# Twelve early loads moved from GpSimd's casting DMA queue to two plain fp32 queues, with the casts on ScalarE and VectorE

## The chip, the core and the metric

The kernel runs on one core of a Trainium2 chip. The metric is the time of one execution in microseconds of device time; lower is better. The core's engines run side by side, each through its own list of instructions in order: TensorE (PE, the matmuls), VectorE (DVE), ScalarE (ACT), GpSimd (POOL) and SyncE (SP). Sixteen DMA engines move data between the chip's main memory and the core. A transfer is started by an instruction on SP, ACT or POOL and goes through that engine's queue. In the profile q0 is POOL's queue, q1 SP's and q10 ACT's.

## What is computed

Retention (attention without a softmax, with a decay by distance) for 8 batches and 8 heads, and a feed-forward network with an exact GELU on its result:

```python
# q, k, v: (8, 8, 576, 64) fp32; w_in: (512, 2048), w_out: (2048, 512)
scores = scale * np.matmul(q, k.transpose(0, 1, 3, 2))
gamma = 1.0 - 2.0 ** (-5.0 - np.arange(H, dtype=np.float32))
Dmat = np.where(rel >= 0, gamma[:, None, None] ** rel[None, :, :], 0.0)
attn = np.matmul(scores * Dmat[None], v)
x = attn.transpose(0, 2, 1, 3).reshape(4608, 512)
h = x @ w_in
g = 0.5 * h * (1.0 + erf(h * inv_sqrt2))
out = g @ w_out
```

## The kernel before

The 4,608 rows of `x` are worked in 36 *units*. A unit is a chunk of 128 positions of one batch with all its heads (the last, short chunks of two batches share a unit). Four units make a block of 512 rows. For each unit the kernel loads q, k and v as bfloat16, turns q and k (`turn`: PE transposes, line 457), forms the scores (`scores`), multiplies them with the decay mask on VectorE (`masked`), multiplies by v (`inner`) and copies the result into a tile `x` (`evacuate`). Across chunks a state is carried (`state`, `cross`). For each block follow the first matmul with `w_in` and the GELU (`mlp1`, `mlp1_fast`) and the second with `w_out` (`mlp2`, `mlp2_fast`). Nearly all matmuls are recorded on line 453, the helper `mm`.

The order of all instructions is fixed when the program is built. A planner in the kernel keeps an estimated clock for each engine (`T`), estimated landing times of loads (`land`, `land_in`, `land_out`), and at each step picks work that is ready by these estimates. On the chip each engine then runs its list in that order and waits on semaphores where an input is not there. Where the planner expects PE to wait, early in the run, it puts in matmuls on a tile of zeros (`warm`, the first ten of them ahead of the loop) that fill the time.

The first four units (chunk 0 of batches 0 to 3) are special: their q, k and v go into slices of one tile, `early`, each [128, 512] bfloat16, and they come first. In the kernel before, three of these twelve tiles (q, k, v of unit 0) are loaded as fp32 at the very start, by SP (q32, first_v) and ACT (k32), line 147, into buffers that later hold outputs (`o_sb`), and are cast to bfloat16 by instructions: q on VectorE (line 1220), k and v on ScalarE (line 1223). The other nine are issued by POOL (line 369), whose DMA casts on the way.

POOL's queue carries nearly everything: `load` issues one item, and the list `ORDER` gives the items' order. `wi0` to `wi7` are the eight chunks of `w_in` (256 columns each, line 311), `wo0` to `wo7` the eight chunks of `w_out` (line 326), `q4` the q of unit 4, `n` a second layout of k, `dq` a table made on POOL, `io` the two iotas of the constants. `sw_dma` is the planner's estimate for POOL's queue: at most eight transfers in flight, each with an issue time and a time to move.

The constants at the top of the kernel steer the planner: how far scores may run ahead of the MLP (`AHEAD`, `RATE`), when units are joined (`JOIN`, `LEAD`, `NEAR`), when the first states and a mask are made (`STATE10`, `MSK_AT`).

Of the kernel before, what the change touches and what calls it, by code (L numbers as in the profile page):

```python
# [9 lines left out]
FP32 = mybir.dt.float32  # L10
# [7 lines left out]
def kernel(  # L18
# [14 lines left out]
    nc = tc.nc  # L33
    ctx.enter_context(tc.manual_schedule())

    B, H, S, D = q.shape
# [5 lines left out]
    C = 128  # L42
# [10 lines left out]
    units = [(bp, 0, j) for bp in range(2) for j in range(2)]  # L53
# [23 lines left out]
    N_LK = 4  # L77
# [4 lines left out]
    N_VH = 4  # L82
    VH_ACT = [4, 22, 1]
    N_XB = 4
    AHEAD = 8
    RATE = 5.6
    STORE_AT = 62.0
    CROWD = 66.0
    STATE10 = 36.0
    HOT = 8.0  # L90
    FETCH = 5.0
    ARRIVE = 5.6
    WARM_TO = 24.0
    JOIN = 1
    JOIN_SB = 0.0
    VISIT = 4
    LEAD = 3.0
    NEAR = 1.4
    SLACK, SB, PER_G, PER_B, TURN0 = 1.2, 2.0, 8.0, 20.0, 0.0
    FINE = 0.38  # L100
    FPOOL = 0.6
    N_V = 6
    V0_HW = 1
    N_WARM = 10
    MSK_AT = 20.0
    HK = N_DF // 2

    const = ctx.enter_context(tc.tile_pool(name="const", bufs=1))
    ld_pool = ctx.enter_context(tc.tile_pool(name="ld", bufs=1))
# [5 lines left out]
    o_pool = ctx.enter_context(tc.tile_pool(name="o", bufs=4))  # L115
# [3 lines left out]
    T = dict.fromkeys(("pe", "act", "dve", "pool", "sp"), 0.0)  # L119
# [22 lines left out]


    first = {}
    for nm, src, eng in (("q32", q, nc.sync), ("k32", k, nc.scalar), ("first_v", v, nc.sync))[:2 + V0_HW]:
        t = first[nm] = o_pool.tile([128, H, D], FP32, tag="o_sb", name=nm)
        eng.dma_start(t, src[0, :, 0:C, :].rearrange("h s d -> s h d"))
    zeros = ld_pool.tile([128, 512], BF16, tag="v", bufs=N_V, name="zeros")
    nc.vector.memset(zeros, 0.0)
    lgh = const.tile([128, H, 1], FP32, name="lgh")  # L150
# [81 lines left out]
    sw = [0.0]  # L232
# [3 lines left out]
    land = {}  # L236
    loaded = {}
    land_in, land_out = {}, {}

    def sw_dma(issue, move):  # L240
        if len(flying) >= 8:
            T["pool"] = max(T["pool"], flying[-8])
        at = T["pool"]
        T["pool"] += issue
        sw[0] = max(sw[0] + move, at + ARRIVE + move - 0.9)
        flying.append(sw[0])
        return sw[0]

# [55 lines left out]
    def load(what, i):  # L304
        if what == "io":
            constants()
            return
        if what == "v" and i == 0 and V0_HW:
            return
        if what == "wi":  # L310
            nc.gpsimd.dma_start(w_in[:, :, i * 256:(i + 1) * 256],  # L311
                                moe_w_in[:, i * 256:(i + 1) * 256].rearrange("(c p) f -> p c f", p=128))
            land_in[i] = sw_dma(0.79, 1.35)
            return
        if what == "dq":
            at, by = (i - 1, step) if i else (1, back)
            assert at in dq_done
            dq_done.add(i)
            finish_later()
            n = min(C, S - i * C)  # L320
            nc.gpsimd.tensor_tensor(dqT[:, i, :, 0:n], dqT[:, at, :, 0:n],
                                    by.to_broadcast([128, HP, n]), op=ALU.mult)
            on("pool", 1.2, 0.0, True)
            return
        if what == "wo":
            nc.gpsimd.dma_start(w_out[:, 2 * i:2 * i + 2, :],
                                moe_w_out[i * 256:(i + 1) * 256, :].rearrange("(c p) f -> p c f", p=128))
            land_out[i] = sw_dma(0.75, 1.36) + 0.5
            return
        if group_of[i] in BY_PE and what == "n":  # L330
            return
        bp, ci, j = units[i]
        qk, v_ld, kn = tiles_of(i)
        if what in "qk" and group_of[i] in BY_PE:
            dst = qk["qk".index(what)].rearrange("p (h e j d) -> p e h j d", h=HP, e=2, j=2)[:, :, :, j]
            for e in range(2):
                nc.gpsimd.dma_start(dst[:, e], {"q": q, "k": k}[what][2 * bp + j, HP * e:HP * e + HP, ci * C:ci * C + C, :].rearrange("h s d -> s h d"))
                land[what, i] = sw_dma(FPOOL, 0.48)
            return
        if what in "qk" and group_of[i] in BY_DVE:  # L340

            n = C if j is not None else TAIL
            per = n // 32 * D
            for jj in (j,) if j is not None else range(2):
                for e in range(2):
                    p0 = 64 * e + 32 * jj
                    nc.gpsimd.dma_start(qk["qk".index(what)][p0:p0 + 32, 0:HP * per].rearrange("p (h x) -> p h x", h=HP),  # L347
                                        {"q": q, "k": k}[what][2 * bp + jj, HP * e:HP * e + HP, ci * C:ci * C + n, :]
                                        .rearrange("h (b t) d -> b h (t d)", b=32))
                    land[what, i] = sw_dma(FPOOL, FINE) if j is not None else sw_dma(FPOOL, FINE / 2)  # L350
            return
        if what == "n":
            nc.gpsimd.dma_start(kn.rearrange("p j e h d -> p (j e h) d"),
                                k[2 * bp:2 * bp + 2, :, ci * C:ci * C + C, :].rearrange("b h s d -> s (b h) d"))
            land[what, i] = land[what, i + 1] = sw_dma(1.27, 1.8)
            return
        if what == "v" and i >= 4 and j is not None:
            nc.gpsimd.dma_start(v_ld.rearrange("p j h d -> p (j h) d"),  # L358
                                v[2 * bp:2 * bp + 2, :, ci * C:ci * C + C, :].rearrange("b h s d -> s (b h) d"))
            land[what, i] = land[what, i + 1] = sw_dma(1.27, 1.8)  # L360
            return
        src = {"q": q, "k": k, "v": v}[what]
        for jj in (j,) if j is not None else range(2):
            n = C if j is not None else TAIL
            if what == "v":
                dst = v_ld if i < 4 else v_ld[:, j] if j is not None else v_ld[n * jj:n * jj + n, 0]
            else:
                dst = qk["qk".index(what)] if i < 4 else qk["qk".index(what)][0:n, :, jj]
            nc.gpsimd.dma_start(dst, src[2 * bp + jj, :, ci * C:ci * C + n, :].rearrange("h s d -> s h d"))
            land[what, i] = sw_dma(0.88, 0.9) if j is not None else sw_dma(0.68, 0.5)  # L370

    tiles_of(0)
    land["q", 0], land["k", 0] = 4.85, 5.5
    if V0_HW:
        land["v", 0] = 6.8
    cast_due = {("q", 0): (loaded[0][0][0], first["q32"]), ("k", 0): (loaded[0][0][1], first["k32"])}
    if V0_HW:
        cast_due["v", 0] = (loaded[0][1], first["first_v"])
    ORDER = ("wi7 io wi0 q1 k2 wi1 k1 k3 v0 v1 q2 wo2 q3 wi5 v2 wo0 wi2 wi3 wi6 v3 wo3 wo4 wi4 wo5 wo1 wo6 n4 q4 "
             "wo7 k4 dq2 v4 k5 q5 q6 q8 q7 k6 k7 v8 v6 k8 k9 q10 n8 n6 k10 k11 q9 dq3 q11 k12 dq0 k13 q12 v12 v10 "  # L380
             "dq4 n10 n12 q13").split()

    def next_order():
        item = ORDER.pop(0)
# [828 lines left out]
    def fire():  # L1213
        now = T["pe"]
        while ORDER and T["pool"] <= now + 1.5:
            next_order()
        for key in [x for x in cast_due if land[x] <= now + 0.2]:
            dst, src = cast_due.pop(key)
            if key[0] == "q":
                nc.vector.tensor_copy(dst, src)  # L1220
                land[key] = on("dve", 0.66, land[key]) + 0.05
                continue
            nc.scalar.copy(dst, src)
            land[key] = on("act", 0.6, land[key]) + 0.05
            if key[0] == "k":
                more_constants()
        while later:
            n = next((n for n, x in enumerate(later) if x[0] <= now and T[x[1]] <= now + 0.05), None)
            if n is None:
                break  # L1230
            _, engine, dur, fn = later.pop(n)
            fn()
            on(engine, dur, now)
        if FAST2 and not wt and not wsum and len(land_out) == N_DF // 2 and max(land_out.values()) <= now and {0, 1, 2, 3} <= s_done:
            wsum.extend(w_out_sums())
        while cast_u and cast_u[0][0] <= now + 0.1:
            state_cast()
        while apart_due and apart_due[0][1] <= now + 0.1 and T["act"] <= now + (0.5 if apart_due[0][0] > group_of[min(nA, N_U - 1)] else 3.0):
            apart()
        while True:  # L1240
            jobs = side_jobs(now)
            if not jobs:
                break
            min(jobs, key=lambda x: x[0])[1]()
        while stores and max(stores[0][0], STORE_AT if stores[0][1] == 0 else 0.0) <= now + 0.2:
            put()
# [52 lines left out]
    for _ in range(N_WARM):  # L1299
        b, t = bank([128, 512], FP32, "warm")  # L1300
# [149 lines left out]
```

## Time and profile before

| | |
|---|---|
| time, median of 2 runs | 290.36 us (289.91 to 290.81) |
| the profiled execution's own time | 290.68 us |
| its span, first to last instruction | 288.8 us |
| PE busy | 279.9 us, 97% |
| DVE, ACT, POOL busy | 228.3, 181.1, 140.8 us |
| POOL's DMA queue | 21.12 MB in 100,528 packets |
| SP's and ACT's DMA queues | 9.51 and 0.72 MB |
| granted clock | 1.000 |

Busy times are sums over the whole span. PE's share includes the matmuls on zeros. A line in the timeline has the start, the length, the engine, the line of the kernel, what is written and read with shapes, the count, and in brackets the idle time before it and what ended it. A DMA queue's row has the number of its packets in the window asked for, their megabytes, and the time that they took as a share of the sixteen engines' time; packets of one queue overlap, so the share can pass 100%.

### The profile page before, as it was taken

The numbers are of one execution on the slowest core, as the hardware profiler recorded it, in microseconds if no ns is written. First come the engines' busy times: TensorE is split into PE (matmuls) and PEld (weight loads), VectorE is DVE, ScalarE is ACT, GpSimd is POOL, SyncE is SP. The second block draws the span as 40 slices with busy tenths as digits, with TensorE's granted clock in tenths as the row PEclk, the third lists the DMA queues.
The fourth block names the chain that finished last, engine by engine and source line by source line (L and its number), as shares of the span: only waits on it lengthen the run. The fifth ranks groups of instructions, "written<-read, shape, count | busy, mean of one in ns | idle before, by whom it ended". The sixth has DMA issues, their size and how long they took to land.

```text
span 288.8 us, 9857 instructions
## 1 busy us (share of the span) xinstructions
PE 279.9 (97%) x4211; PEld 210.2 (73%) x4216; DVE 228.3 (79%) x386; ACT 181.1 (63%) x406; POOL 140.8 (49%) x213
## 2 busy tenths in 40 slices
PE   7899999999999999999999999999999999999994
PEld 3468768788764566666666666777888888888883
DVE  6473297499795689678997799869999999999861
ACT  7556544895758868777787779664545453556421
POOL 8865799798849967878677774000000000000000
PEclk9999999999999999999999999999999999999999
DMA  9999999979998999999999996311020202202014
GB/s 158 168 189 195 190 157 160 207 85 140 130 148 64 141 170 140 143 139 186 136 169 155 91 160 51 76 39 39 2 75 0 76 2 74 75 0 75 36 57 128
DMA packets 109260, 31.97 MB, mean 111 GB/s; under 512 B 85920, under 2 KB 104864, under 8 KB 109216
## 3 DMA queue, kind: packets, MB, share of 16 engines
q0 software_dynamic: 100528, 21.12, 83.3%
q1 hardware_dynamic: 7264, 9.51, 10.3%
q10 hardware_dynamic: 1424, 0.72, 0.9%
q8 instruction: 33, 0.54, 0.8%
q14 instruction: 11, 0.09, 0.1%
HBM read 42.99 MB, written 9.44 MB: 182 GB/s over the span
## 4 chain that ended last, share of the span: by engine, by line
PE 92%; DMA 2%; DVE 2%; issue 1%; POOL 1%; ACT 0%; POOLq 0%; DVEq 0%
PE psum L453 91%; DMA early<-in_q_dram 2%; PE psum L457 1%; DVE x L788 1%; POOL w_in L311 1%; DVE qT L551 0%; DVE u_sb L710 0%; ACT u_acc L712 0%; ACT x L490 0%; DVE u_acc L715 0%; DVE qkT L488 0%; DVE o_sb L904 0%; POOL val L185 0%; POOL pos L187 0%; POOLq L185 0%
## 5 line engine op out<-in xcount | busy, mean ns | idle before, releaser
L453 PE MATMUL psum<-x,w_in 128*128 128x256 bf16 (+2 forms) x784 | 118.3, 297 | 1.3 <-issue 0.5
L453 PEld LDWEIGHTS <-w_in 128*128 128x128 bf16 x784 | 68.8, 98 | 29.4 <-issue 2.5
L453 PEld LDWEIGHTS <-g_all 128*128 128x128 bf16 x576 | 55.4, 98 | 13.9
L453 PE MATMUL psum<-w_out,g_all 128*128 128x256 bf16 (+1 forms) x438 | 58.4, 280 | 0.2
L819 ACT ACTIVATE g_all<-psum 128x512 bf16<-128x512 f32 x64 | 37.6, 595 | 19.3 <-PE psum L453 17.9
L347 POOL DMA_DIRECT2D k_ld<-in_k_dram x64 | 35.0, 564 | 23.4 <-DMA kn_ld<-in_k_dram 11.6
L453 PEld LDWEIGHTS <-s 128*128 128x128 bf16 x408 | 39.4, 98 | 7.5
L620 DVE TENSOR_TENSOR ret<-psum,msk 128x1024 bf16<-128x1024 f32 (+1 forms) x32 | 35.6, 1149 | 8.7 <-PE psum L453 7.3
L637 ACT ACTIVATE vh<-v_ld,dv 128x128 bf16<-128x128 bf16 (+1 forms) x144 | 42.3, 383 | 0.0
L1033 ACT ACTIVATE g_all<-t 128x512 bf16<-128x512 f32 x36 | 22.7, 632 | 28.2 <-DVE t L1041 28.2
L347 POOL DMA_DIRECT2D q_ld<-in_q_dram x64 | 35.2, 567 | 1.2 <-DMA k_ld<-in_k_dram 1.1
L490 ACT COPY t<-psum 128x256 f32<-128x256 f32 (+1 forms) x47 | 20.3, 434 | 23.6 <-PE psum L453 23.4
L453 PE MATMUL psum<-wt,s 128*128 128x256 bf16 x272 | 33.8, 273 | 0.0
L904 DVE TENSOR_TENSOR o_sb<-psum,t 128x256 f32<-128x256 f32 x51 | 21.4, 421 | 11.2 <-PE psum L453 5.8
L1041 DVE TENSOR_TENSOR t<-psum,t 128x512 f32<-128x512 f32 x36 | 24.6, 688 | 2.7 <-ACT t L490 1.1
L822 ACT ACTIVATE g_all<-psum 128x512 bf16<-128x512 f32 (+1 forms) x42 | 20.0, 494 | 7.9 <-PE psum L453 7.1
L488 DVE COPY t<-psum 128x512 f32<-128x512 f32 (+1 forms) x40 | 22.1, 563 | 1.1 <-PE psum L453 1.1
L453 PE MATMUL psum<-x,ws 128*128 128x256 bf16 x144 | 19.5, 273 | 0.0
L453 PE MATMUL psum<-wt,g_all 128*128 128x256 bf16 x136 | 17.5, 273 | 0.0
L453 PE MATMUL psum<-w_out,s 128*128 128x256 bf16 x136 | 17.5, 273 | 0.0
L358 POOL DMA_DIRECT2D v_ld<-in_v_dram x14 | 16.4, 1179 | 2.0 <-issue 0.9
L562 ACT COPY q_ld<-qT 128x1024 bf16<-128x1024 bf16 (+1 forms) x16 | 15.0, 936 | 3.8 <-DVE qT L551 3.0
(102 smaller groups left out, 329.6 us busy)
## 6 DMA issues: line engine op xcount, KB each, us to landing
out_dram<-o_sb SPq DMA_DIRECT2D x31, 256.0 KB, 3.7
q_ld<-in_q_dram POOLq DMA_DIRECT2D x56, 64.0 KB, 5.3
k_ld<-in_k_dram POOLq DMA_DIRECT2D x56, 64.0 KB, 4.9
v_ld<-in_v_dram POOLq DMA_DIRECT2D x14, 256.0 KB, 5.3
kn_ld<-in_k_dram POOLq DMA_DIRECT2D x12, 256.0 KB, 6.9
w_in<-in_moe_w_in_dram POOLq DMA_DIRECT2D x8, 256.0 KB, 8.8
w_out<-in_moe_w_out_dram POOLq DMA_DIRECT2D x8, 256.0 KB, 9.5
q_ld<-in_q_dram POOLq DMA_DIRECT2D x16, 32.0 KB, 4.2
```

Source lines behind the costliest of these rows:

```text
L347: nc.gpsimd.dma_start(qk["qk".index(what)][p0:p0 + 32, 0:HP * per].rearrange("p (h x) -> p h x", h=HP), {"q": q, "k": k}[what][2 * bp + jj ...
L358: nc.gpsimd.dma_start(v_ld.rearrange("p j h d -> p (j h) d"), v[2 * bp:2 * bp + 2, :, ci * C:ci * C + C, :].rearrange("b h s d -> s (b h) d"))
L453: nc.tensor.matmul(*a, **k)
L488: nc.vector.tensor_copy(dst, src)
L490: nc.scalar.copy(dst, src)
L620: nc.vector.tensor_tensor(both.rearrange("p (e h) s -> p e h s", e=2), t, by, op=ALU.mult)
L637: nc.scalar.activation(vh[:, 0:m, h], src[:, :, h], AF.Copy, scale=dv[:, h, ci:ci + 1])
L819: nc.scalar.activation(g_all[:, t % 2, :, m0, :], hT.rearrange("p n (a c) -> p (n a) c", a=2), AF.Gelu)
L822: nc.scalar.activation(g_of(t, 2 * lo // TOK)[:, m0:m0 + n, lo_:lo_ + hi - lo], hT, AF.Gelu)
L904: nc.vector.tensor_tensor(dst, src, f[key], op=ALU.add)
L1033: nc.scalar.activation(g_of(t, part)[:, m0:m0 + 2], src, AF.Gelu)
L1041: nc.vector.tensor_tensor(f[key], f["b"][1], f[key], op=ALU.add)
```

## The change

All twelve tiles of the first four units are loaded as fp32 through SP's and ACT's queues at the start: k0 and k1 on ACT, the ten others on SP in the order q0 v0 q1 v1 k2 q2 v2 k3 q3 v3. Four go into `o_sb` buffers, eight into buffers of the rings `lk` and `v`, which later loads use. Each is then cast by an instruction; the planner gives it to VectorE or ScalarE, whichever it expects to be done first, except for unit 0 (q on VectorE, k and v on ScalarE). POOL's list begins with a chunk of `w_in`, the iotas and more weights, and has no tile of the first four units. The planner takes the twelve landing times from a table, `LANDS`, and lets POOL's transfers take 1.6 times as long (`SHARED`) until the last of them. Several of the planner's constants and the order of the later loads are different too.

```diff
-    AHEAD = 8
-    RATE = 5.6
+    AHEAD = 13
+    RATE = 4.8
...
-    STATE10 = 36.0
+    STATE10 = 32.0
...
-    JOIN = 1
+    JOIN = 2
...
-    LEAD = 3.0
-    NEAR = 1.4
+    LEAD = 5.0
+    NEAR = 0.6
...
-    V0_HW = 1
     N_WARM = 10
-    MSK_AT = 20.0
+    LANDS = 4.8, 5.5, 6.6, 7.0, 7.6, 8.4, 9.2, 10.0, 10.8, 11.6, 12.4, 13.2
+    SHARED = 1.6
+    MSK_AT = 24.0
...
     first = {}
-    for nm, src, eng in (("q32", q, nc.sync), ("k32", k, nc.scalar), ("first_v", v, nc.sync))[:2 + V0_HW]:
-        t = first[nm] = o_pool.tile([128, H, D], FP32, tag="o_sb", name=nm)
-        eng.dma_start(t, src[0, :, 0:C, :].rearrange("h s d -> s h d"))
+    for key, eng, pool, tag, bufs in (
+            ("q0", nc.sync, o_pool, "o_sb", 4), ("k0", nc.scalar, o_pool, "o_sb", 4), ("v0", nc.sync, o_pool, "o_sb", 4),
+            ("k1", nc.scalar, o_pool, "o_sb", 4), ("q1", nc.sync, ld_pool, "lk", N_LK), ("v1", nc.sync, ld_pool, "lk", N_LK),
+            ("k2", nc.sync, ld_pool, "lk", N_LK), ("q2", nc.sync, ld_pool, "lk", N_LK), ("v2", nc.sync, ld_pool, "v", N_V),
+            ("k3", nc.sync, ld_pool, "v", N_V), ("q3", nc.sync, ld_pool, "v", N_V), ("v3", nc.sync, ld_pool, "v", N_V)):
+        bp, ci, j = units[int(key[1])]
+        dst = first[key] = pool.tile([128, H, D], FP32, tag=tag, bufs=bufs, name="raw_" + key)
+        eng.dma_start(dst, {"q": q, "k": k, "v": v}[key[0]][2 * bp + j, :, ci * C:ci * C + C, :].rearrange("h s d -> s h d"))
...
-        sw[0] = max(sw[0] + move, at + ARRIVE + move - 0.9)
+        sw[0] = max(sw[0] + move * (SHARED if sw[0] < LANDS[-1] else 1.0), at + ARRIVE + move - 0.9)
...
-    ORDER = ("wi7 io wi0 q1 k2 wi1 k1 k3 v0 v1 q2 wo2 q3 wi5 v2 wo0 wi2 wi3 wi6 v3 wo3 wo4 wi4 wo5 wo1 wo6 n4 q4 "
-             "wo7 k4 dq2 v4 k5 q5 q6 q8 q7 k6 k7 v8 v6 k8 k9 q10 n8 n6 k10 k11 q9 dq3 q11 k12 dq0 k13 q12 v12 v10 "
-             "dq4 n10 n12 q13").split()
+    cast_due = {}
+    for n, key in enumerate(first):
+        i = int(key[1])
+        tiles_of(i)
+        land[key[0], i] = LANDS[n]
+        cast_due[key[0], i] = ({"q": loaded[i][0][0], "k": loaded[i][0][1], "v": loaded[i][1]}[key[0]], first[key])
+    ORDER = ("wi0 io wi7 wi1 wi6 wo2 wi5 wi3 wi4 wo1 wi2 wo3 wo0 wo4 wo5 k4 q4 wo7 q5 wo6 v4 dq2 k5 q6 k7 k6 q7 q8 "
+             "q9 n4 v6 k8 k9 v8 q10 k11 n8 n6 k10 dq3 q11 q12 v10 dq0 q13 dq4 k12 k13 n10 n12 v12").split()
...
-        for key in [x for x in cast_due if land[x] <= now + 0.2]:
+        for key in sorted([x for x in cast_due if land[x] <= now + 0.2], key=lambda x: land[x]):
             dst, src = cast_due.pop(key)
-            if key[0] == "q":
+            if key == ("q", 0) or key[1] and max(T["dve"], land[key]) + 0.7 <= max(T["act"], land[key]) + 0.6:
                 nc.vector.tensor_copy(dst, src)
```

More of the change, by code (lines that the diff above doesn't have):

```diff
@@ L306, in load @@
             constants()
-            return
-        if what == "v" and i == 0 and V0_HW:
             return
@@ L370, in load @@
             land[what, i] = sw_dma(0.88, 0.9) if j is not None else sw_dma(0.68, 0.5)
[L372 to L378, printed above, removed]
-    ORDER = ("wi7 io wi0 q1 k2 wi1 k1 k3 v0 v1 q2 wo2 q3 wi5 v2 wo0 wi2 wi3 wi6 v3 wo3 wo4 wi4 wo5 wo1 wo6 n4 q4 "
-             "wo7 k4 dq2 v4 k5 q5 q6 q8 q7 k6 k7 v8 v6 k8 k9 q10 n8 n6 k10 k11 q9 dq3 q11 k12 dq0 k13 q12 v12 v10 "
-             "dq4 n10 n12 q13").split()
+    cast_due = {}
[6 more added lines that the diff above has]
+             "q9 n4 v6 k8 k9 v8 q10 k11 n8 n6 k10 dq3 q11 q12 v10 dq0 q13 dq4 k12 k13 n10 n12 v12").split()
     def next_order():
@@ L1224, in fire @@
             land[key] = on("act", 0.6, land[key]) + 0.05
-            if key[0] == "k":
+            if key == ("k", 0):
                 more_constants()
```

## The prediction

> **What bounds the kernel now.** I read the page first, then busy time by stage, then the chain that ended last, then the DMA queues in narrow windows around the place where the change acts.
>
> ```profile
> span 288.8 us, 9857 instructions
> PE 279.9 (97%) x4211; PEld 210.2 (73%) x4216; DVE 228.3 (79%) x386; ACT 181.1 (63%) x406; POOL 140.8 (49%) x213
> ```
> ```profile
> 5.40:22.00 16.60, 14.34 (x221) 9.06 (x224) 10.02 (x20) 9.33 (x20) 13.34 (x18) 1.00 1.81 180
> 22.00:50.00 28.00, 27.88 (x440) 21.70 (x442) 15.99 (x28) 14.59 (x36) 23.50 (x32) 1.00 1.72 176
> 50.00:80.00 30.00, 28.61 (x504) 23.76 (x502) 23.35 (x30) 23.91 (x58) 25.94 (x39) 1.00 1.44 144
> 80.00:289.00 209.00, 204.82 (x3042) 154.37 (x3040) 175.58 (x285) 129.46 (x288) 73.74 (x116) 1.00 0.72 91
> ```
> In a stage's row the second number is its length and the third PE's busy time. From 22.0 us PE has hardly a gap until the last stores (1.4 us in 50 to 80): a microsecond lost or won before that reaches the end nearly whole, since nothing later has room to take it up. Before 22 us, PE's busy time is partly filler:
>
> ```profile
> 1.19 4.45 PE L453 MATMUL psum<-zeros 128*128 128x512 bf16 x10 [1.19 <-DVE zeros L149]
> 7.36 1.47 PE L453 MATMUL psum<-zeros 128*128 128x512 bf16 x6
> 11.23 1.50 PE L453 MATMUL psum<-x,w_in 128*128 128x128 bf16 x24
> 19.91 0.40 PE L453 MATMUL psum<-qkT 64*128 64x128 bf16 x8
> 20.24 1.05 PE L453 MATMUL psum<-x,w_in 128*128 128x256 bf16 x8
> ```
> The matmuls on `zeros` only pass time until data come. The chain says what sets this stage: a load of `early`, the bfloat16 q, k, v of the first four units.
>
> ```profile
> 3.31 6.46 DMA early<-in_q_dram
> 22.00 12.11 PE psum L453 x171
> ```
> The run lasted 290.68 us by its own time, 1.88 over the span and 0.32 over the median of the runs shown (290.36). The sum is made on 290.68.
>
> **The change part by part.** Nine loads leave POOL's queue, where each cost 0.9 us of issue:
>
> ```profile
> 12.18 0.89 POOL L369 DMA_DIRECT2D early<-in_v_dram  x1 [0.47 <-DMA w_in<-in_moe_w_in_dram]
> 4.76 0.56 DVE L1220 CAST early<-q 128x512 bf16<-128x512 f32 x1 [0.21 <-DMA q<-in_q_dram]
> 7.57 0.62 ACT L1223 CAST early<-first_v 128x512 bf16<-128x512 f32 x1 [0.66 <-DMA first_v<-in_v_dram]
> ```
> That by itself is worth nothing: by 12 us POOL is so far ahead that it waits for landings, so the 16 DMA engines set the pace. Seven more casts go to ACT and two to DVE, 0.62 and 0.56 us each; both engines were idle for over 6 of the 16.6 us before 22, which hides them, and where a cast stands in front of PE it is counted below. The planner's other constants (`AHEAD`, `RATE`, `LEAD`, `NEAR`, `JOIN`) and the later loads' order move work after 42 us; there PE's gaps of before leave 1.4 us to win, and I take as much to lose and nothing for the sum. The real matmuls have the same columns in all; 15 of the 32 fillers go. So the question is when the tiles land, now that SP's and ACT's queues and POOL's queue are full at once. In before they overlapped for some 2 us only, with `first_v`, and that is the place to read. Rows of a narrow window: queue, packets, MB, share.
>
> ```profile
> q10 hardware_dynamic: 727, 0.19, 81.7%
> q1 hardware_dynamic: 408, 0.10, 45.0%
> ...
> q0 software_dynamic: 195, 0.10, 143.7%
> q1 hardware_dynamic: 6, 0.00, 1.2%
> ...
> q0 software_dynamic: 122, 0.10, 127.9%
> ...
> q0 software_dynamic: 1229, 0.15, 243.3%
> ```
> Alone, SP's and ACT's queues (q1, q10; 3 to 4 us) move 1135 packets of 256 bytes a microsecond, 14 ns for each on each of 16 engines: a 256 KB tile, 64 packets per engine, takes 0.90 us. POOL's queue (q0) nearly alone (7.0 to 7.5 us) moves 195 packets of a w_in chunk in 0.5 us: 41 ns each, 32 per engine and chunk, 1.3 us. From 15.0 to 15.5 us, mostly w_out, it moves 0.10 MB too, so a chunk is again 1.3 us, 81 ns for each of 16 packets. Its tile packets (12 to 13 us) take 13 ns. Now both at once, as the last engine that still has packets of `first_v` works them off: windows 6.75 to 6.98, 6.76 to 6.95 and 6.98 to 7.08 us.
>
> ```profile
> q0 software_dynamic: 89, 0.04, 139.7%
> q1 hardware_dynamic: 4, 0.00, 3.4%
> ...
> q0 software_dynamic: 75, 0.04, 142.8%
> q1 hardware_dynamic: 2, 0.00, 2.0%
> ...
> q0 software_dynamic: 37, 0.02, 133.1%
> q1 hardware_dynamic: 7, 0.00, 7.3%
> ```
> Four q1 packets fit into 0.23 us but only two into the 0.19 inside it, so three spacings are over 0.19 and under 0.23: 63 to 77 ns, where 14 would do alone. In the next 0.1 us seven pass, 14 ns apart: there that engine's POOL ring paused between two transfers. So on a shared engine the queues alternate packet by packet: one 256-byte packet of q1, one 512-byte packet of q0, 14 + 41 = 55 ns of work and some 12 for the turn. A tile on SP's queue then takes 64 turns x 67 ns = 4.3 us, not 0.90. The changed kernel's table of landings (`LANDS`) steps by 0.8 us.
>
> SP's queue holds q0 v0 q1 v1 k2 q2 v2 k3 q3 v3, ACT's k0 k1. POOL's packets begin shortly before 5 us; rows of 0 to 5, 4 to 5, 5.0 to 5.5 and 5.5 to 6.0 us:
>
> ```profile
> DMA packets 2777, 0.71 MB, mean 142 GB/s; under 512 B 2757, under 2 KB 2777, under 8 KB 2777
> q0 software_dynamic: 20, 0.01, 1.5%
> ...
> DMA packets 899, 0.23 MB, mean 231 GB/s; under 512 B 879, under 2 KB 899, under 8 KB 899
> ...
> q0 software_dynamic: 83, 0.04, 61.8%
> ...
> q0 software_dynamic: 152, 0.08, 113.6%
> ```
> I take 5.2 us as the start on a middle engine. In before two tiles and part of a third had moved by 5 us, with q10 already dry; with both queues kept full at 1135 a microsecond from 4 us on (1,878 by then: 2777 less the 899 of 4 to 5 us) it is some 3,240 packets by 5.2 us: q0 and k0 whole and 37 of 64 per engine of v0 and k1. To the end of v3 SP's queue has 27 + 8 x 64 = 539 packets per engine left, each beside one packet of POOL's. In POOL's new order those 539 are eight w_in chunks (256), six of w_out (96), k4 and q4 (128), wo7 (16) and part of q5 (43). Turns: 256 x 67 ns = 17.2; 112 x (81 + 14 + 12 = 107) = 12.0; 171 x (13 + 14 + 12 = 39) = 6.7; together 35.8 us. The pause seen between two POOL transfers gives q1 some six packets more; over 17 such pauses that is at most 2.2 us saved, of which I take half. Landing: the last q1 packet passed before 7.08 us and its cast began at 7.57, 0.5 us. And three rows for what follows v3:
>
> ```profile
> 11.88 1.28 ACT L822 ACTIVATE g_all<-psum 128x256 bf16<-128x256 f32 x3 [0.69 <-PE psum L453]
> 18.31 0.60 ACT L490 COPY qkT<-psum 128x512 bf16<-128x512 bf16 x1
> 21.21 0.41 PE L453 MATMUL psum<-ret,early 128*32 128x128 bf16 x16
> ```
> So v3 is there at 5.2 + 35.8 - 1.1 + 0.5 = 40.4 us; without the 12 ns a turn at 5.2 + 14.1 + 10.6 + 4.6 + 0.5 = 35.0; without the pauses 41.5. On the way q1 lands near 11, v1 16, k2 20, q2 25, v2 31, k3 35 and q3 37, and PE, which runs in order, waits for each.
>
> What is queued behind v3: on ACT its cast (0.62), two gelus (0.43 each), and then the `qkT` copy (0.60) that PE's scores of unit 3 need, some 1.8 us with overlaps. So PE runs without a gap from 42.2 us. What it has done by then, by the built order: all 32 turns, three scores, three inner products, 56 narrow and 8 wide matmuls on w_in. Before had at 22.0 the same 32 turns, three inner products, a score more (0.4 us), and 48 narrow and 8 wide: equal within 0.2 us. The end moves by 42.2 - 22.0 = 20.2 us: 290.68 + 20.2 = 310.9, so 311. By the bounds of v3's landing 305.5 to 312.
>
> One cost has no place in that sum: the first ten fillers took 0.445 us each, the six at 7.36 us 0.245. If PE falls back to that pace after gaps of 4 us and more, 4.45 us at half pace cost up to 2.2 us: 314. Below nothing it can't go. I take none, as PE works in pieces from 37 us on. The Trainium skill (TensorE: Matmul & The Clock Gate, Part 1: The HAM clock gate) has the clock halve after an idle window of about 3.4 us; no run here shows a gap that long yet.
>
> **The rivals.** *SP's queue gets two packets a turn.* In the rows above the count per turn was one, against one size only; with w_out's longer packets it could be other. Then v3 needs 270 POOL packets: 238 x (41 + 28 + 11 = 80 ns) + 32 x 120 = 22.8 us, landing at 28.5, PE free at 30.3, end + 8.3: 299. The Trainium skill (DMA: Bandwidth & Descriptors, Queues, rings and completion order) says that an engine drains a whole packet of some 9 to 17 descriptors of one ring before it turns to the next. As an estimate by that page, 16 of SP's against 4 KB of POOL's would come out as this rival; spacings of 63 to 77 ns over four packets speak against it.
>
> *The tiles come first, as `LANDS` has it.* If SP's queue gets four or more packets a turn, v3 is there by 20.2 us, from where the change costs nothing on this chain. At best, 12,288 packets at 1135 a microsecond, it lands near 14; but then POOL's first w_in chunk lands near 15, and PE's new order has matmuls on w_in ahead of unit 2's turns, which takes most of the gain back. With both as planned, the 15 fillers (15 x 0.245 = 3.7 us) would be saved: 287; with weights late 294; I take 290. For it speaks that SP's queue starts over 2 us ahead of POOL's; against it the tail of `first_v`, and that the plan's twelve tiles and four chunks by 13.2 us are 4.2 MB in some 11 us, where the fullest microsecond above (q1 and q10, 3 to 4 us) has 0.29 MB.
>
> That the loads are not issued early is no rival: SP's four last ones wait only for landings near 5 to 8 us.
>
> **How the numbers follow.** One packet a turn 0.78 (own range 305 to 314); two a turn 0.12 (299); tiles first 0.10 (287 to 294). A measurement of this kernel tells about 2% from no change, 5.8 us. The first two are slower by more than that, 0.90; of the third I give 0.08 to within 2% and 0.02 to faster. The range, 299 to 316, reaches down to the second case and up to the half-pace cost with 2 us for the later order.
>
> **What would show it.** Right: v3's cast near 40 us on ACT; w_in chunks landing 2.1 us apart instead of 1.3; PE gaps of 4 to 8 us before the turns of units 1 and 2 and the scores of unit 3; gapless PE from some 42 us; from there on the distance between the two kernels stays. Wrong: tiles landing under 2 us apart, or v3's cast before 21 us. If v3 lands at 40 and the end moves by much less than 20, my step that nothing later takes it up is wrong.

## The result, and the profile after

The changed kernel takes 316.52 us, the median of 2 runs (315.59 to 317.46), against 290.36: a ratio of 1.090 (95% interval 1.075 to 1.106), 26.2 us slower. The profiled execution is the one of 315.59 us, 24.9 us over the profiled one of before. First its span, PE's busy time and granted clock, then busy time by stage; in a stage's row the second number is its length, the third PE's busy time, and the one behind POOL's counts PE's granted clock.

```profile
span 313.8 us, 9791 instructions
PE 282.6 (90%) x4169; PEld 213.0 (68%) x4169; DVE 233.6 (74%) x388; ACT 181.2 (58%) x405; POOL 133.7 (43%) x204
...
PEclk9555769999999999999999999999999999999999
```
```profile
5.40:22.00 16.60, 7.23 (x62) 3.63 (x62) 5.89 (x12) 4.60 (x10) 6.62 (x10) 0.56 1.34 188
22.00:46.00 24.00, 10.87 (x155) 9.10 (x156) 5.20 (x10) 7.49 (x17) 13.41 (x17) 0.59 1.49 179
46.00:80.00 34.00, 32.04 (x472) 24.85 (x470) 24.95 (x34) 18.38 (x37) 28.36 (x40) 1.00 1.31 121
80.00:313.80 233.80, 228.68 (x3474) 174.07 (x3472) 193.93 (x307) 147.35 (x336) 81.06 (x128) 1.00 0.71 89
```
The loss is in the first 46 us: PE is busy for 18.1 of 40.6 us there. The DMA engines are not idle meanwhile (188 and 179 GB/s, as before). ACT's timeline shows for what the other engines wait, each tile's cast behind its landing (in brackets the idle time and what ended it):

```profile
12.91 0.62 ACT L1225 CAST early<-raw_q 128x512 bf16<-128x512 f32 x1 [4.55 <-DMA raw_q<-in_q_dram]
17.75 0.62 ACT L1225 CAST early<-raw_v 128x512 bf16<-128x512 f32 x1 [4.22 <-DMA raw_v<-in_v_dram]
...
34.02 0.62 ACT L1225 CAST early<-raw_v 128x512 bf16<-128x512 f32 x1 [6.57 <-DMA raw_v<-in_v_dram]
...
43.44 0.62 ACT L1225 CAST early<-raw_v 128x512 bf16<-128x512 f32 x1 [2.78 <-DMA raw_v<-in_v_dram]
44.51 0.59 ACT L492 COPY qkT<-psum 128x512 bf16<-128x512 bf16 x1
```
The last row but one is v3. PE's timeline has the gaps that come of it:

```profile
13.58 1.04 PE L459 MATMUL psum<-ident,early 128*128 128x128 bf16 x8 [5.21 <-ACT early L1225]
19.39 0.61 PE L455 MATMUL psum<-qkT 64*128 64x128 bf16 x8 [2.41 <-ACT qkT L492]
27.50 1.03 PE L459 MATMUL psum<-ident,early 128*128 128x128 bf16 x8 [6.11 <-ACT early L1225]
38.27 0.61 PE L455 MATMUL psum<-qkT 64*128 64x128 bf16 x8 [6.28 <-DVE qkT L490]
...
41.06 2.76 PE L455 MATMUL psum<-x,w_in 128*128 128x128 bf16 x24
45.54 0.40 PE L455 MATMUL psum<-qkT 64*128 64x128 bf16 x8
```
From the scores of unit 3 at 45.54 us on PE has hardly a gap. The DMA queues of three windows (9.5 to 14.5 us beside w_in, 27.5 to 31.5 beside w_out, 34.5 to 37.5 beside tile pieces) show the mechanism itself; rows are queue, packets, MB, share:

```profile
q0 software_dynamic: 1223, 0.61, 88.2%
q1 hardware_dynamic: 1221, 0.31, 46.6%
...
q0 software_dynamic: 638, 0.62, 91.3%
q1 hardware_dynamic: 634, 0.16, 30.0%
...
q0 software_dynamic: 1267, 0.16, 80.4%
q1 hardware_dynamic: 1251, 0.32, 79.3%
```
One packet of SP's queue goes for one of POOL's, whatever its size. A turn is 5.0 x 16 / 1222 = 65 ns, 4.0 x 16 / 636 = 101 ns and 3.0 x 16 / 1259 = 38 ns; the prediction had 67, 107 and 39.

### The profile page after: what moved, and what is told of

The parts are those of the page before. It is cut to its first block, busy times and chain, and to the rows that moved or that the text cites. A ratio compares the mean times of both kernels' runs of the same rounds, so it can differ in the third digit from the quotient of the medians.

```text
span 313.8 us, 9791 instructions
## 1 busy us (share of the span) xinstructions
PE 282.6 (90%) x4169; PEld 213.0 (68%) x4169; DVE 233.6 (74%) x388; ACT 181.2 (58%) x405; POOL 133.7 (43%) x204
## 4 chain that ended last, share of the span: by engine, by line
PE 68%; DMA 17%; POOL 8%; issue 4%; DVE 1%; ACT 1%; POOLq 0%; DVEq 0%
PE psum L455 68%; DMA v_ld<-in_v_dram 5%; DMA k_ld<-in_k_dram 5%; DMA w_in<-in_moe_w_in_dram 5%; DMA q_ld<-in_q_dram 2%; POOL q_ld L351 2%; POOL k_ld L351 2%; POOL w_in L315 1%; POOL v_ld L362 1%; POOL dqT L325 1%; POOL kn_ld L357 1%; POOL q_ld L341 0%; DVE ret L622 0%; ACT q_ld L564 0%; DVE x L794 0%
## 5 line engine op out<-in xcount | busy, mean ns | idle before, releaser
L455 PE MATMUL psum<-x,w_in 128*128 128x256 bf16 (+2 forms) x752 | 121.8, 309 | 1.6 <-issue 1.4
L455 PEld LDWEIGHTS <-w_in 128*128 128x128 bf16 x752 | 70.9, 101 | 29.1 <-issue 2.8
L455 PE MATMUL psum<-w_out,g_all 128*128 128x256 bf16 (+1 forms) x440 | 59.3, 281 | 0.0
L824 ACT ACTIVATE g_all<-psum 128x512 bf16<-128x512 f32 (+1 forms) x38 | 19.2, 530 | 6.7 <-PE psum L455 6.4
L790 DVE TENSOR_TENSOR x<-psum,dqT 128x1024 bf16<-128x1024 f32 (+1 forms) x15 | 17.0, 1145 | 2.0 <-ACT g_all L821 1.4
L455 PE MATMUL psum<-wt,g_all 128*128 128x256 bf16 x136 | 17.5, 273 | 0.0
L455 PE MATMUL psum<-w_out,s 128*128 128x256 bf16 x136 | 17.5, 273 | 0.0
```

The source lines that it names most:

```text
L455: nc.tensor.matmul(*a, **k)
L824: nc.scalar.activation(g_of(t, 2 * lo // TOK)[:, m0:m0 + n, lo_:lo_ + hi - lo], hT, AF.Gelu)
```

## The experiments

The theory: a tile of SP's queue advances by one packet for each packet of POOL's queue, and the lateness of the tiles is the loss. Rivals: SP's queue is slow by itself; the planner's constants cost the time; the order, planned for landings that don't come, costs more than the lateness. The time of the kernel before on the same chips was 291.11 us (the two holds, the true landings, the constants), 290.80 (smaller packets, two queues, 44 fillers, the planned hold) and 291.77 (both edits, 128 fillers); each ratio is against its own.

**Weights held back behind q2.** GpSimd touches one column of q2 before its first weights; all else stays in its order, except that GpSimd's two iotas now come ahead of the first chunk.

```diff
+            nc.gpsimd.tensor_tensor(held_, first["q2"][:, 0, 0:1], first["q2"][:, 0, 0:1], op=ALU.mult)
+            load_w_in(0)
```


> The changed kernel with every engine's order as it is, but POOL's first weight chunk waits for q2's landing (a one-column product on POOL reads that tile). My theory, that SP's queue and POOL's alternate packet by packet on each DMA engine: without POOL's packets beside them the tiles land 0.9 us apart, q2 near 10 us, and v3 near 14 instead of 43.4; the first w_in chunk lands some 6.3 us after its issue, near 17. PE stops once, at its first matmul on w_in, and runs from about 17.5 us with 5.4 us less real work done than before had at 22: about 292 us, 290 to 296. First rival, that SP's queue is slow of itself (small packets, one queue, issues of up to 4.6 us): the tiles stay 4.3 us apart, and the weights come only after q2 at 27 us: over 316. Second rival, that the later order and the planner's constants cost the time: no change, 314 to 318.

Measured: 297.87 us (297.38 to 298.43), ratio 1.0226 (1.0205 to 1.0247). ACT's timeline, then the DMA queue from 8 to 13 us, with no packet of POOL's in it:

```profile
10.34 0.62 ACT L1232 CAST early<-raw_v 128x512 bf16<-128x512 f32 x1 [0.57 <-DMA raw_v<-in_v_dram]
...
12.77 0.62 ACT L1232 CAST early<-raw_q 128x512 bf16<-128x512 f32 x1 [0.32 <-DMA raw_q<-in_q_dram]
13.97 0.62 ACT L1232 CAST early<-raw_v 128x512 bf16<-128x512 f32 x1 [0.59 <-DMA raw_v<-in_v_dram]
```
```profile
q1 hardware_dynamic: 4322, 1.09, 134.9%
```
Without POOL's packets v1 is cast at 10.34 us, not 17.75, and a tile takes 1.2 us, not 4.3: SP's queue isn't slow by itself. That is 19 us of the 26 back by one wait. The time is over the 290 to 296 that were expected. The rate here is 864 packets/us and not the 1135 of the prediction, so q2 lands at 12.7 us and the weights are asked for 3 us later than I had reckoned. But PE's first product with w_in begins only 0.9 us behind the 17.5 expected:

```profile
18.44 1.04 PE L462 MATMUL psum<-x,w_in 128*128 128x128 bf16 x8 [4.13 <-DMA w_in<-in_moe_w_in_dram]
```
The rest of the miss lies behind that row. PE works at half clock there (0.50 from 16 to 22 us, 0.73 from 22 to 28), waits 0.76 us for the next chunk, and comes to the scores of unit 3, the point that stands for 22.0 us in the kernel before, at 28.82 us, where 22.9 (17.5 + 5.4) was reckoned. From there to the end it is 266.8 us, exactly as in the kernel before from 22.0: the whole loss of this kernel is ahead of 28.82 us, and the later order of loads, which is the changed kernel's, costs nothing in it.

**Weights held back behind v3.** The same edit on the last tile.

> The same, but POOL's first weight chunk waits for v3, the last tile. My theory: all twelve tiles 0.9 us apart, v3 near 14 us, first w_in chunk near 20; the end 3 to 4 us after that of the kernel that waits for q2: 294 to 299. First rival (SP's queue slow of itself): v3 at 43 us or later and no weight before 49: 325 or more. Second rival (later order): 314 to 318.

Measured: 304.2 us in one run, over the 294 to 299 expected and well under both rivals (314 to 318, 325 or more). PE waits 8.05 us for w_in, up to 21.72 us. The weights start 4.6 us later than in the kernel above (v3's landing against q2's), and the time is 6.3 us longer, with up to 2 us of that in a wait for "issue" as the fillers' experiment shows them below: tiles first is no way out either, the price moves to the weights.

**The true landings in the table.** `LANDS` gets the landings measured in the changed kernel, and nothing else is edited, so the planner makes another order.

```diff
-    LANDS = 4.8, 5.5, 6.6, 7.0, 7.6, 8.4, 9.2, 10.0, 10.8, 11.6, 12.4, 13.2
+    LANDS = 4.8, 5.5, 7.7, 9.0, 12.9, 17.7, 21.9, 26.8, 34.0, 37.1, 39.5, 43.4
```


> The changed kernel with the twelve landing times that its own profile showed in the planner's table (7.7 for v0 up to 43.4 for v3), so that the planner gives PE other work while tiles are late; the loads and queues are as they are. My theory and the first rival: the tiles land as late as in the changed kernel, within 1 us, but PE has the first and second matmul of units 0 and 1 to do meanwhile, up to 10 us of work more: 303 to 311. If the time stays at 316, the late tiles cost it all whatever the order; if it falls to 295 or below, the order was the cause and not the lateness.

Measured: 302.42 us (302.04 to 302.80), ratio 1.0382 (1.0358 to 1.0406). The stages of its profile:

```profile
5.40:22.00 16.60, 12.60 (x164) 6.93 (x167) 6.54 (x13) 8.29 (x17) 6.62 (x10) 1.00 1.34 188
22.00:46.00 24.00, 17.98 (x260) 13.35 (x266) 7.99 (x17) 10.79 (x24) 13.31 (x17) 0.99 1.48 180
```
The tiles come as late as ever and the DMA moves the same, but PE, given other work or fillers ahead of the late tiles, gets 260 matmuls into 22 to 46 us (none of them a filler) in place of 155, at a granted clock of 0.99 in place of 0.59. Against their own kernels before, the losses are 11.3 and 26.2 us: some 15 of the 26 us are not the lateness but an order that waits for it, and 11 us are left of the lateness.

**The constants alone.** Before's loads and order, with the changed kernel's `AHEAD`, `RATE`, `JOIN`, `LEAD`, `NEAR`, `STATE10` and `MSK_AT`.

> The loads of the kernel before (three tiles on SP and ACT, nine on POOL, its list of loads) with the other constants of the changed kernel (AHEAD, RATE, STATE10, JOIN, LEAD, NEAR, MSK_AT). My theory: within 2 us of before, 289 to 293. Second rival, that the constants and the later order cost the time: 300 or more.

Measured: 291.70 us (290.85 to 292.97, 10 runs), ratio 1.0023 (1.0002 to 1.0043). The constants are not the loss. The later loads' order is not in this kernel; the one with the weights behind q2 has it.

**Smaller packets of POOL's.** Each w_in chunk as two DMAs of 128 columns.

```diff
-            nc.gpsimd.dma_start(w_in[:, :, i * 256:(i + 1) * 256],
+            for f in (2 * i, 2 * i + 1):
+                nc.gpsimd.dma_start(w_in[:, :, f * 128:(f + 1) * 128],
```


> The changed kernel with each w_in chunk moved by two DMAs of 128 columns, so that its packets have 256 bytes and not 512; everything else, and the order on every engine, as in the changed kernel. Theory (one SP packet for one POOL packet): a turn beside w_in shrinks from 67 ns to about 19 + 24 = 43 ns, so a tile beside w_in takes 64 turns of 43 ns = 2.75 us, not 4.3, although a w_in chunk now takes 2.75 us, not 2.15. Then v1 lands near 14, q2 near 20 and v3 near 32.5 us (43.4 in the changed kernel), and the time is 303 to 311 us, most likely 306. Rival (the two queues share by bytes, or POOL's queue goes first): the tiles keep their landings or come later, v3 at 43 or more, and the time is 314 to 322 us.

Measured: 308.18 us (307.33 to 310.70), ratio 1.060 (1.052 to 1.067). Queues from 15 to 17 us, and the cast of v3:

```profile
q0 software_dynamic: 681, 0.17, 83.9%
q1 hardware_dynamic: 675, 0.17, 64.2%
```
```profile
35.78 0.62 ACT L1226 CAST early<-raw_v 128x512 bf16<-128x512 f32 x1 [2.15 <-DMA raw_v<-in_v_dram]
```
Still one for one, 2.0 x 16 / 678 = 47 ns a turn (43 expected). Halving the packet of a queue that has nothing to do with the tiles brings v3 7.7 us sooner and the end 8.3. v3 is 3.3 us later than expected; longer turns are some of that (4 ns over the turns beside w_in), the rest I come back to below.

**Tiles on two queues.** k2, v2, k3 and v3 go to ScalarE's queue; the last three are issued behind early casts.

```diff
-            ("k2", nc.sync, ...), ("v2", nc.sync, ...), ("k3", nc.sync, ...), ("v3", nc.sync, ...)
+            ("k2", nc.scalar, ...), ("v2", nc.scalar, ...), ("k3", nc.scalar, ...), ("v3", nc.scalar, ...)
...
             nc.scalar.copy(dst, src)
+            if key in put_off:
+                nc.scalar.dma_start(*put_off.pop(key))
```


> The changed kernel with k2, v2, k3 and v3 on ScalarE's queue and no longer on SyncE's: k2 issued at the head, v2, k3 and v3 each behind an early cast on ScalarE; the order of all other work is unchanged. Theory (the queues of SyncE, ScalarE and GpSimd take turns packet by packet, so that two of three packets are tile packets): a turn of three beside w_in is about 67 + 19 = 86 ns and brings two packets of tiles, so v3 lands near 32 us, not 43.4, the weights come some 5 us later than in the changed kernel, and the time is 302 to 310 us, most likely 306. Rival (SyncE's and ScalarE's queues share one turn against GpSimd's): tiles land as late as in the changed kernel, v3 at 42 or more, 313 to 318 us.

Measured: 306.26 us (302.75 to 307.22), ratio 1.049 (1.041 to 1.058). Queues from 10 to 20 us, and v3's cast:

```profile
q0 software_dynamic: 1898, 1.07, 73.9%
q1 hardware_dynamic: 1898, 0.48, 36.1%
q10 hardware_dynamic: 1895, 0.48, 21.4%
```
```profile
31.75 0.62 ACT L1229 CAST early<-raw_v 128x512 bf16<-128x512 f32 x1 [0.36 <-DMA raw_v<-in_v_dram]
```
Three queues, one packet each: a turn of 10.0 x 16 / 1897 = 84 ns brings two tile packets, and v3 is there 11.7 us sooner. The rival (SP and ACT share one turn) falls.

**Both edits.** Tiles on two queues and the weights behind q2.

> Both edits in one: k2, v2, k3 and v3 on ScalarE's queue, and GpSimd's first weights held back behind q2. Theory (two queues without GpSimd's packets move 1135 packets/us, one only 850, so q2 is there near 10.5 us in place of 12.7 and the weights begin 2 us sooner; what is left of the loss behind the hold is that start): v3 near 15 us, first w_in chunk near 16, 294 to 297 us. Rival (the queues of SyncE and ScalarE together are no faster than one, or the later weights cost nothing): 297 to 299.5 us.

Measured: 299.48 us (298.08 to 302.22), ratio 1.029 (1.022 to 1.036). The theory falls on its premise; queues from 7 to 13 us:

```profile
q1 hardware_dynamic: 2918, 0.74, 75.8%
q10 hardware_dynamic: 2263, 0.57, 59.0%
```
Together 5181 packets in 6.0 us, 864 per us: exactly what SP's queue moved alone. Two queues get a larger share against POOL's, but no more out of the DMA engines. Without POOL's packets beside them the two don't alternate one for one: from 7 to 8 us SP's queue moved 782 packets and ACT's 76, from 8 to 9 us 68 and 793. q2 shares that rate with ACT's tiles now and is cast at 13.92 us, so the weights start 1.2 us later, not sooner.

**Fillers against the half pace.** In the kernel with the weights behind q2, 44 matmuls of zeros ahead of the first product with w_in, and then 128 narrower ones.

```diff
+            for _ in range(44):
+                nc.tensor.matmul(hT[:, 0, :], lhsT=zeros[:, :128], rhs=zeros[:, 0:hi - lo], start=True, stop=True)
```


> The kernel with the weights held back behind q2, with 44 matmuls of zeros (128x128) on TensorE just ahead of the first x,w_in product, where it waits 4.1 us for the first chunk; their result is overwritten. Theory (the half pace behind the wait costs 1 to 3 us, which the prediction took as nothing): the first x,w_in products run at 0.50 us for 8 in place of 1.04, and the time falls from 297.9 to 295 to 297 us. Rival (TensorE waits for chunks then, so that its pace costs nothing): 297.5 to 298.5 us.

> The kernel with the weights held back behind q2, with 128 matmuls of zeros (128x64) ahead of the first x,w_in product in place of the 44 wider ones; their result is overwritten. With 44, TensorE waited 1.70, 3.16 and 1.98 us for nothing but its own instructions at 71, 172 and 196 us, where without them such waits add up to 1.5 us. Theory (the inserted instructions shift the places where TensorE's instructions are fetched, which the program's order allows for in pieces of 256, and 128 matmuls with their 128 weight loads are just one piece): the waits are gone and the half pace too, 294.5 to 297 us. Rival (any instructions that are put in cost this, or the fillers do so in another way): 302 to 308 us.

Measured: 305.75 us (304.89 to 308.21), ratio 1.052 (1.043 to 1.061), and 298.96 us (296.91 to 301.28), ratio 1.024 (1.017 to 1.031). With 44 the time went up by 8 us, where a gain was expected. The fillers did not do what they were put in for. The 44 were through at 16.2 us, PE waited 3.30 us more, and the first product behind that wait ran at half pace as before:

```profile
13.58 2.62 PE L824 MATMUL psum<-zeros 128*128 128x128 bf16 x44
19.50 1.02 PE L462 MATMUL psum<-x,w_in 128*128 128x128 bf16 x8 [3.30 <-DMA w_in<-in_moe_w_in_dram]
```
With 128 the first product took 0.62 us, and the second, behind a wait of 1.20 us, 1.03 again. PE's timeline also shows waits for nothing in the profile, far behind the edit; the fourth row is from the kernel with 128:

```profile
70.97 0.41 PE L462 MATMUL psum<-q_ld,u_sb 32*64 32x128 bf16 x25 [1.70 <-issue]
172.06 0.45 PE L462 MATMUL psum<-q_ld,u_sb 32*64 32x128 bf16 x33 [3.16 <-issue]
195.54 0.29 PE L462 MATMUL psum<-q_ld,u_sb 32*64 32x128 bf16 x9 [1.98 <-issue]
```
```profile
173.74 1.97 PE L462 MATMUL psum<-x,w_in 128*128 128x512 bf16 x5 [2.69 <-issue]
```
All such waits together are 7.1 us with 44 fillers and 2.0 without, 5.1 of the 8 us. The first three rows fall in runs of very short matmuls. That 128 matmuls with their weight loads, a whole piece of 256 instructions, cost 7 us less than 44 points to the place in the instruction stream, as the kernel's own helper `place` has it (it counts instructions in pieces of 256). The DMA rows point the same way: one 16 KB packet of the profile's queue of instructions (q8) begins at 68.6, 169.4, 193.3 and 171.4 us, and PE goes on 2.2 to 2.7 us behind each. That the wait is the fetching itself is argued from this; no run takes the fetching away.

The half pace can be priced from these traces in one place. From the second chunk's product to the scores of unit 3, the same instructions take 7.73 us without fillers (21.09 to 28.82, with one wait of 0.22) and 6.30 with 44 (22.02 to 28.32), where the clock is full sooner: some 1.2 us. The second chunk came 0.9 us later in that run, so only 0.5 us of it was left at that point. What the half pace costs in all stays open: neither filler brought the time under that of the kernel without.

**The hold, planned.** The weights behind q2, and the planner told of it: the landings measured there, `SHARED` 1.0, POOL busy until 12.9 us.

> The kernel with the weights held back behind q2, but the program's planner is told it: the twelve landings measured in that kernel (4.9 to 17.5 us) in LANDS, SHARED 1.0, and GpSimd busy until 12.9 us. Theory (what is left of the loss behind the hold is a plan made for other landings, and the weights' 3 us later start): 290 to 295 us. Rival (what is left is the later weights alone, and no order helps): 296 to 299 us.

Measured: 298.88 us (296.39 to 299.57; one run more took 301.18), ratio 1.024 (1.015 to 1.033). That is no better than without the plan (1.0226), which speaks for the rival: what is left behind the hold is the later weights. It is not shown, though, as PE waited only 0.90 us for w_in in the profiled execution, behind fillers, and 2.6 us for q_ld later. No version beat the kernel before.

## Why the prediction was right and wrong

*Direction and mechanism held.* One packet for one, with a turn set by POOL's packet: read from four packets in 0.23 us of the kernel before, it came out at 65, 101 and 38 ns over thousands of packets, and smaller packets and a third queue moved it as they should. Two packets a turn and tiles first are both out. The statement of the Trainium skill (DMA: Bandwidth & Descriptors, Queues, rings and completion order) that a ring is drained for some 9 to 17 descriptors before the next has its turn isn't what these queues do here: 1898, 1898 and 1895 packets in the same 10 us are equal numbers a turn, with the two tile queues at 256 bytes a packet and the weights at 512 and 1024. That the number is one shows at the end of v3, where one engine alone still has packets of it: three windows of 0.2 us from 42.4 to 43.0 us hold 5 of SP's packets each, one every 40 ns.

*The term that was mis-sized: v3's landing, 40.4 us predicted, 43.44 measured, and over the upper bound of 41.5 too.* The turns were, if anything, a little shorter than predicted. What failed is what they were multiplied with and lessened by:

- The packets that SP's queue moved by 9.5 us. The prediction carried the 1135 packets/us of 3 to 4 us on and came to 3,240 by 5.2 us, half of them on each queue. Rows of 0 to 5.2 us, and of 6.5 to 7.5:

```profile
q1 hardware_dynamic: 1715, 0.44, 42.1%
q10 hardware_dynamic: 1090, 0.28, 25.4%
...
q0 software_dynamic: 237, 0.12, 87.5%
q10 hardware_dynamic: 254, 0.06, 46.1%
q1 hardware_dynamic: 19, 0.00, 3.6%
```
  2,805 had moved: the high rate is that of the opening alone, behind it 864 is the sustained one. It was ACT's queue that was behind, with 1,090; SP's had its half and more, 1,715. But ACT's k1 then had more left to move, and from 6.5 to 7.5 us SP's queue moved 19 packets while k1's moved. From 5.2 to 9.5 us SP's queue came to 768 packets, 48 per engine, where the prediction has 4.3 / 0.067 = 64 turns. From 9.5 us to v3's landing it still had 7,917 packets (495 per engine; a tile has 1,040, 65 per engine and not 64), where the prediction has 539 less 64 = 475: 20 turns of 67 ns, 1.3 us.
- The pauses. I took 1.1 us off for the places where POOL's ring stops between transfers. It didn't stop in the steady stretch: the counts of the two queues are equal to within 1.3% in all three windows. 1.1 us.
- The rest, 0.6 us, is what a second hole in SP's queue, 38 to 39 us, and one late engine cost, less what the shorter turns gave. The hole, and a row of 27.5 to 34 us:

```profile
q0 software_dynamic: 349, 0.18, 131.9%
q1 hardware_dynamic: 62, 0.01, 11.5%
...
q8 instruction: 1, 0.02, 0.9%
```
  From 38.45 to 39.06 us SP's queue moved 16 packets, one every 38 ns: one engine still had packets of q3, and v3's began only about 39.1 us. The first hole stands at the end of a tile too (2,061 of the first two tiles' 2,080 packets were through at 6.5 us), and so does one in the kernel with smaller packets, from 13 to 14 us, whose v3 was late as well. Why the next tile's packets wait there no experiment told; it stays open. One engine was also behind at v3's own end (the 5 packets in each 0.2 us above). The row of q8 may be why: one packet of instructions took 0.9% of sixteen engines' 6.5 us, some 0.9 us of a single engine. That it was the same engine is not shown.

*From v3 to PE:* 1.8 us predicted, 2.1 measured (43.44 to 45.54): PE had 24 matmuls on w_in at 2.76 us, 1.50 at full pace, and so was still at the eight wider ones behind them (44.30 to 45.61) when `qkT` was there at 45.10. So of the half-pace cost that I put at nothing, bounded by 2.2, some 0.4 us reached the end. The granted clock is 0.56 and 0.59 in the stages with gaps of 4 us and more; the Trainium skill (TensorE: Matmul & The Clock Gate, Part 1: The HAM clock gate) has it halve after an idle window of about 3.4 us, and the gaps and the clock of these stages agree. Half pace was there before the first such gap, though:

```profile
7.76 0.61 PE L455 MATMUL psum<-zeros 128*128 128x512 bf16 x1
```
In the kernel before, one such filler took 0.38 us (at 6.35 us). Ahead of this one PE had waited 0.47, 0.62 and 0.52 us and was busy for 0.79 of the 2.0 us from 5.2 to 7.2: a stretch that was partly idle was enough.

*What follows v3.* From the scores of unit 3 to the end it is 268.3 us (313.8 - 45.54), in the kernel before 266.8 from 22.0: 1.5 us that I took as nothing, mostly one wait for a copy on DVE:

```profile
67.47 0.63 PE L455 MATMUL psum<-q_ld,kT 32*128 32x128 bf16 x32 [1.75 <-DVE kT L490]
```
It is not the later order by itself: with the weights behind q2, every engine's later instructions in the same order take 266.8 us from that point on.

*The sum.* 20.2 predicted + 3.0 (landing) + 0.3 (to PE) + 1.5 (later) = 25.0, against 24.9 between the two profiled executions. The median lies 0.9 over the profiled one since the other run took 317.46; with two runs I can't say why. In kernels of this study a wait for "issue" at one place near 172 us was 0.51 us in one profile (weights behind q2) and 3.01 in another (both edits), which would be enough.

*The order, taken as given.* The prediction asked when PE may go on in the built order, and did not ask what another order would make of the same landings. The experiment with the true landings says that this was over half of the loss: the same late tiles cost 11 us when the order knows of them. The sum was made for the order as built, so this changes no term of it.

*A remark that failed.* The prediction had SP's last four issues wait only for landings near 5 to 8 us. SP was done with v3's issue at 34.55 us. As v3's packets began at about 39.1, this does not seem to have set its landing.

## What to carry to other kernels

When a load moves to another queue, count packets, not bytes: GpSimd's queue and SyncE's (with ScalarE's as a third) alternated one packet for one here, so a queue of small packets gets on at the pace of the other's large ones, and a second queue bought a larger share but no more throughput. Read rates from a long window and not from the opening microsecond. In a kernel whose order is planned ahead from a table of landings, a wrong table can cost more than the lateness itself, so measure the landings first.

## What the runs showed of the hardware that I had not expected

- SP's and ACT's loads with 256-byte packets move at 1135 packets/us (287 GB/s) for about one microsecond at the start and at 864 (218 GB/s) from then on, alone or together. A tile through SP's queue then takes 1.2 us; the casting load that it replaces moved 1,229 packets in a microsecond, 0.83 us a tile. The change made each of nine tiles dearer for the DMA engines.
- SP's issue instructions seem to wait for room in the queue: k2's took 3.74 us, v3's 7.74 in the changed kernel, against 1.14 for most of those behind k2 where the weights were held back. In the changed kernel v2's, k3's, q3's and v3's were done at 17.95, 22.62, 26.76 and 34.55 us, and the tile three places ahead of each on SP's queue was cast from 17.75, 21.95, 26.83 and 34.02.

```profile
5.25 3.74 SPq L153 DMA_DIRECT2D raw_k<-in_k_dram  x1
...
26.81 7.74 SPq L153 DMA_DIRECT2D raw_v<-in_v_dram  x1
```
- 88 instructions put into PE's list early were followed by waits of 1.70, 3.16 and 1.98 us some 50 to 180 us later, each ending 2.2 to 2.7 us after a 16 KB packet of instructions began to move; 256 left one, of 2.69 us.
